# One order for all engines, made by a list scheduler in the source, and fp32 turns of the first four tiles on TensorE

## The chip, the cores and the metric

The kernel runs on one core of a Trainium2 chip. The core has five engines with a queue each: TensorE (PE), VectorE (DVE), ScalarE (ACT), GpSimd (POOL) and SyncE (SP), which here issues the DMAs. The metric is the device time of one execution in microseconds (us), the median of several runs.

## What is computed

```python
def _attn_ref(q, k, v, n_global, n_local):            # B, H, S, D = 4, 8, 768, 64
    scores = np.matmul(q, k.transpose(0, 1, 3, 2)) / np.sqrt(D)
    ...
    is_global = pos[None, :] < int(n_global)           # 8 keys
    is_local = (rel >= 0) & (rel < int(n_local))       # the last 96 keys
    ...
    scores = np.where(is_global | is_local, scores + bias, -1e9)
    a = softmax(scores)
    return np.matmul(a, v)

def _moe_ref(x, g_ln, w_ch1, w_ch2):                   # x: 4 x 768 x 512
    xn = (x - mu) / np.sqrt(var + 1e-06) * g_ln
    return x + np.maximum(xn @ w_ch1, 0.0) @ w_ch2     # 512 -> 2048 -> 512
```

A row sees at most the key block of 128 before its own, its own, and the first 8 keys. The two weight matrices come as 64-bit floats (16 MB together). Everything runs in fp16 pairs of a high and a low part, three products for each full one.

## The kernel before

The 3072 rows are 24 tiles of 128 (`TILES`): t = 0 to 3 are the first blocks of the four batches ("short" tiles, one key block, two groups of four heads), t = 4 to 23 the others ("long" tiles, two key blocks, four groups of two heads). Two tiles make a chunk of the feed-forward net (`CT`), 12 chunks in all.

For a tile, `keys`, `queries` and `values` load 256 KB each, split it (ACT writes the high part, DVE or POOL the low one) and turn k and q with DMA transposes; q is also copied with its halves swapped. A group then goes through `scores` (PE), `reduce` (DVE: mask and row maximum), `exps` (ACT), `turned` (DVE or ACT high part, POOL or DVE low part, then a DMA transpose into `pT`) and `weights_by_values` (PE, tile `pv`). `divide` and the three parts of `norm` make x and its normed fp16 pair, which a DMA transpose turns into `xT`.

`ffn1(c, f)` is one step of 24 matmuls of 256 columns for two of the 16 blocks of the hidden layer, followed by `high` (ACT) and `low` (DVE) into a tile `h`; `ffn2` is a step of 12 matmuls of 512 columns. There are 96 of each, 192 in all. `weight` turns a piece of 1 MB (16 pieces, 8 for each matrix, staging tile `st`) into fp16: ACT at L189, DVE at L190, ACT at L191, DVE at L192, ACT at L194 for the high part, DVE at L195 for the low one.

Until chunk 2 begins, the program orders the work loosely: `run` mixes generators by rates (L624 `f1w` for chunk 0 with the weights of the first matrix, L639 chunk 1, L641 `ffn2_first` for chunks 0 and 1 with the weights of the second matrix and the first 12 groups of long tiles), `ORDER` adds some dependences to DMAs, and the compiling framework arranges each engine's instructions by its own simulated times. From chunk 2 on (L651), `Lane` chains each engine's instructions in the order of the source; there the loop at L656 to L690 puts one group of attention into every second step, and `settle(LAG)` holds the products of weights by values back until two younger groups have been issued. In the profile all instructions of that part show the line of the helper, L90. DMAs are issued on SP in all parts.

Of the kernel before, what the change touches and what calls it, by code (L numbers as in the profile page):

```python
# [23 lines left out]
P = 128  # L24
# [49 lines left out]

@with_exitstack
def banded(ctx, tc, q, k, v, n_global, n_local, g_ln, w1, w2, out, flag):
    nc = tc.nc
    lanes = {}

    class Lane:  # L80
# [33 lines left out]
    marks = {}  # L114

    def mk(key, ins):

        marks[key] = ins
        if ORDER.get(key) in marks:
            tc.add_manual_dep(ins.ins, marks[ORDER[key]].ins.name, NOSYNC, reason="order")  # L120

    place = {bi: t for t, bi in enumerate(TILES)}

    def short(b, i, shape, dtype, tag, name, bufs):

        if 0 < place[b, i] < 2 * CT and not (b, i) in again:
            return hpool.tile(shape, dtype, tag="h", name=name)
        return p2.tile(shape, dtype, tag=tag, name=name, bufs=bufs)

    again = set()  # L130

    def own(b, i, name):
        if place[b, i] < CT and not (b, i) in again:
            return hpool.tile([P, H, P], F16, tag="h", name=f"{name}{b}_{i}")
        return p2.tile([P, H, P], F16, tag=name if i else name + "0", name=f"{name}{b}_{i}", bufs=3 if i else 2)

    def fetch(src, name, b, i):
        f = short(b, i, [P, H, D], F32, "ld", f"{name}f{b}_{i}", 6)
        mk(f"L{place[b, i]}", load.dma_start(out=f, in_=src[b, :, i * P:(i + 1) * P, :].rearrange("h p d -> p h d")))
        return f  # L140

    early = {}

    def loads(t, names):
        for name in names:
            early[name, t] = fetch({"k": k, "q": q, "v": v}[name], name, *TILES[t])

    loads(0, "kq")

    def piece(src, name):  # L150
        st = p3.tile([P, 2, 512], I64, tag="st", name="st" + name, bufs=3)
        mk("D" + name, load.dma_start(out=st, in_=src))
        return st

    def piece1(j, c):
        return piece(w1[2 * c * P:2 * (c + 1) * P, j * 512:(j + 1) * 512].rearrange("(a p) n -> p a n", a=2), f"1_{j}_{c}")

    cnt = counts(tc, const, load, n_global, n_local)
    ng, nl = cnt[:, 0:1], cnt[:, 1:2]

    loads(0, "v")

    mask0 = const.tile([P, H, P], BF16, name="mask0")
    mask1 = const.tile([P, H, 2, P], BF16, name="mask1")
    rel = hpool.tile([P, 2, P], F32, tag="h", name="rel")
    pool.iota(rel, pattern=[[-P, 2], [-1, P]], base=P, channel_multiplier=1, allow_small_or_imprecise_dtypes=True)
    col = hpool.tile([P, P], F32, tag="h", name="col")
    pool.iota(col, pattern=[[1, P]], base=0, channel_multiplier=0, allow_small_or_imprecise_dtypes=True)  # L170
# [5 lines left out]
    w2l = const.tile([P, NF, DM], F16, name="w2l")  # L176
    big = const.tile([P, NF], F32, name="big")
    less = const.tile([P, 1], F32, name="less")
    pool.memset(less, -0.5001)
    wm = const.tile([P, 16], F32, name="wm")  # L180

    def weight(st, dh, dl, name, n):

        words = st.rearrange("p a n -> p (a n)").bitcast(I32).rearrange("p (n two) -> p n two", two=2)
        lo, hi = words[:, :, 0], words[:, :, 1]
        mk("A" + name, act.activation(out=lo, in_=st.rearrange("p a n -> p (a n)").bitcast(U32).rearrange("p (n two) -> p n two", two=2)[:, :, 0], func=AF.Relu, scale=2.0 ** -29, bias=less))  # L189
# [736 lines left out]
```

## Time and profile before

| | us |
|---|---|
| median of three runs | 673.61 (673.53 to 678.36) |
| the profiled execution | 676.25 |
| its span, first to last instruction | 674.5 |
| TensorE busy in it | 586.6 (87%) |

The span is that of the profiled execution; the execution's own time has 1.75 us more around it, and is 2.64 us above the median. Busy time of PE is modelled, since matmuls overlap: the distance from one matmul's start to the next tells what one costs.

### The profile page before, as it was taken

To read this page: it belongs to the slowest core of one execution; us is meant where nothing else is said; L and a number is where in the kernel's file an instruction comes from. 1 tells how busy PE (TensorE), PEld (TensorE's weight loads), DVE (VectorE), ACT (ScalarE), POOL (GpSimd) and SP (SyncE) were. 2 spreads that over 40 slices of the span, in tenths; PEclk is the share of its full clock that TensorE was granted. 3 is DMA by queue.
4 is the path that set the end of the run, shared out by engine and by line. 5 is a ranking of instruction groups with operands and counts; after the bars stand their busy time and mean duration, and the time that the engine had idled before them with its cause. 6 is when DMAs were issued, how large, how long until landed. Compare 5 with 4: busy or idle time off the path is not lost.

```text
span 674.5 us, 13418 instructions
## 1 busy us (share of the span) xinstructions
PE 586.6 (87%) x5218; PEld 415.1 (62%) x5218; DVE 414.0 (61%) x984; ACT 289.5 (43%) x752; POOL 145.0 (22%) x133
## 2 busy tenths in 40 slices
PE   1113698989798998999999999999999999999995
PEld 0002565865495586587587587596686695784852
DVE  5778898845665655556475475466466457555640
ACT  4877986643144334244254243353344343230110
POOL 0000011522222332222232232233233223200000
PEclk9999999999899998999999999999999999999998
DMA  9999798996548776766886877778786785321001
GB/s 214 240 255 299 138 267 247 175 180 103 133 79 142 151 153 105 142 142 113 149 161 118 150 125 127 141 134 162 129 161 107 140 142 115 75 48 32 17 0 36
DMA packets 265767, 93.51 MB, mean 139 GB/s; under 512 B 255456, under 2 KB 255456, under 8 KB 265696
## 3 DMA queue, kind: packets, MB, share of 16 engines
q1 hardware_dynamic: 265696, 92.57, 68.8%
q8 instruction: 43, 0.70, 0.4%
q14 instruction: 28, 0.23, 0.1%
HBM read 37.49 MB, written 6.29 MB: 65 GB/s over the span
## 4 chain that ended last, share of the span: by engine, by line
PE 52%; DVE 15%; DMA 13%; ACT 8%; issue 6%; SPq 4%; POOL 1%; ACTq 0%; DVEq 0%; POOLq 0%
PE f L90 42%; DMA qf<-in_q_dram 4%; DMA st<-in_moe_w_ch_dram 4%; PE s L90 3%; SPq L90 3%; PE f L532 2%; ACT T L90 2%; PE pv L90 2%; DVE T L90 2%; DMA vf<-in_v_dram 2%; ACT T L388 1%; DVE st L190 1%; DVE st L192 1%; DVE x L90 1%; ACT st L189 1%
## 5 line engine op out<-in xcount | busy, mean ns | idle before, releaser
L90 PE MATMUL f<-xT,w1h 128*128 128x256 f16 x1280 | 216.7, 275 | 5.4 <-DMA xT<-xn 4.2
L90 PE MATMUL f<-w2h,h 128*128 128x512 f16 x640 | 201.1, 379 | 0.0
L90 PE MATMUL f<-xT,w1l 128*128 128x256 f16 x640 | 176.1, 275 | 0.0
L90 PEld LDWEIGHTS <-h 128*128 128x128 f16 x960 | 90.3, 98 | 97.8
L90 POOL TENSOR_TENSOR pn<-T,pn 128x512 f16<-128x512 f32 x68 | 80.6, 1185 | 301.0 <-DVE pn L90 175.7
L90 PEld LDWEIGHTS <-w1h 128*128 128x128 f16 x1280 | 122.6, 99 | 20.3 <-DMA xT<-xn 4.2
L90 PE MATMUL f<-w2l,h 128*128 128x512 f16 x320 | 121.3, 379 | 0.0
L90 ACT ACTIVATE h<-f 128x512 f16<-128x512 f32 x80 | 46.9, 588 | 80.0 <-PE f L90 79.7
L90 ACT ACTIVATE mn<-nm 128x2 f32<-128x2 f32 x68 | 13.8, 203 | 146.8 <-DVE nm L90 146.8
L90 DVE CAST pn<-T 128x512 f16<-128x512 f32 x68 | 29.1, 427 | 75.4 <-ACT T L90 75.4
L90 ACT ACTIVATE T<-T,mn 128x256 f32<-128x256 f32 x136 | 68.0, 500 | 4.5 <-ACT mn L90 0.4
L90 PEld LDWEIGHTS <-w1l 128*128 128x128 f16 x640 | 63.1, 99 | 7.8
L90 DVE SCALAR_TENSOR_TENSOR h<-f,h 128x512 f16<-128x512 f32 x80 | 55.0, 687 | 20.3 <-ACT h L90 19.5
L90 DVE CUSTOM_DVE_ANT_0 T<-s,mask 128x256 f32<-128x256 f32 x136 | 51.7, 417 | 23.8 <-PE s L90 23.3
L370 PE MATMUL s<-kT,qT 128*128 128x128 f16 x160 | 15.7, 255 | 36.6 <-DMA qT<-qn 27.7
L90 PE MATMUL s<-kT,qT 128*128 128x128 f16 x544 | 42.0, 219 | 6.1 <-DVE kT L90 5.6
L90 DVE SCALAR_TENSOR_TENSOR qn<-qf,qn 128x512 f16<-128x512 f32 x16 | 11.1, 692 | 58.8 <-ACT qn L90 58.8
L90 PEld LDWEIGHTS <-qT 128*128 128x128 f16 x544 | 35.8, 98 | 15.5 <-issue 7.6
L510 PE MATMUL f<-xT,w1h 128*128 128x256 f16 x128 | 36.1, 282 | 10.2 <-DMA xT<-xn 6.2
L90 PEld LDWEIGHTS <-pT 128*128 128x128 f16 x840 | 34.0, 98 | 9.3 <-DMA pT<-pn 0.9
L532 PE MATMUL f<-w2h,h 128*128 128x512 f16 x128 | 39.6, 379 | 0.0
L370 PEld LDWEIGHTS <-qT 128*128 128x128 f16 x160 | 12.5, 115 | 40.3 <-DMA qT<-qn 28.8
(129 smaller groups left out, 824.5 us busy)
## 6 DMA issues: line engine op xcount, KB each, us to landing
st<-in_moe_w_ch_dram SPq DMA_DIRECT2D x16, 1024.0 KB, 6.9
kf<-in_k_dram SPq DMA_DIRECT2D x27, 256.0 KB, 4.1
vf<-in_v_dram SPq DMA_DIRECT2D x27, 256.0 KB, 3.5
qf<-in_q_dram SPq DMA_DIRECT2D x24, 256.0 KB, 4.3
out_dram<-x SPq DMA_DIRECT2D x24, 256.0 KB, 2.4
qT<-qT SPq DMA_DIRECT2D x46, 128.0 KB, 2.5
pT<-pn SPq DMA_TRANSPOSE x88, 3.5
kT<-kn SPq DMA_TRANSPOSE x27, 3.4
```

The costliest lines, as they stand in the source:

```text
L90: ins = getattr(self.engine, name)(*args, **kw)
L189: mk("A" + name, act.activation(out=lo, in_=st.rearrange("p a n -> p (a n)").bitcast(U32).rearrange("p (n two) -> p n two", two=2)[:, :, 0 ...
L190: vec.scalar_tensor_tensor(out=lo, in0=hi, scalar=SIGN, in1=lo, op0=ALU.bitwise_and, op1=ALU.bitwise_or)
L192: vec.scalar_tensor_tensor(out=hi, in0=hi, scalar=3, in1=lo, op0=ALU.logical_shift_left, op1=ALU.bitwise_or)
L370: last = chain(last, pe.matmul(ps[:, u, n_ * P:(n_ + 1) * P], lhsT=qT[a][:, h, :], rhs=use[n_][0][:, h, :], start=(a == 0), stop=(a == 1)))
L388: act.activation(out=T[:, u, :], in_=T[:, u, :], func=AF.Exp, scale=-1.0, bias=mn[:, h:h + 1], accum_out=sm[:, h:h + 1])
L510: last = chain(last, pe.matmul(ps[:, a], lhsT=w1h[:, kk, fs], rhs=xT[:, kk, :], start=(kk == 0), stop=False))
L532: return [pe.matmul(ps, lhsT=hh[:, a, tok], rhs=w, start=(f == 0 and n_ == 0), stop=(f == NF - 1 and n_ == 2)) for n_, (a, w) in enumerate ...
```

## The change

All instructions up to the closing checks are made into tasks with an engine, a cost, the tasks they come after, a rank and the buffers they hold. `Plan.order` lays them out by these costs, always the task that can start first, and among those of one engine that start within 0.05 us the lowest rank; the instructions are then emitted in that order, and `Lane` chains them on each engine from the first one on. `ORDER`, `RATE`, `LAG`, `settle` and the generators are gone.

Beside the order, these parts differ:

- Tiles 0 to 3 (`quick`): k and q are turned in fp32 by PE with an identity, four 128x128 transposes in one PSUM bank (`turn`), and ACT and DVE split them as they leave PSUM; their scores then take four products over 64 rows in place of two over 128. The softmax weights of these tiles and their normed rows are turned likewise. No DMA transpose and no swapped copy of q is left for these tiles (20 turns by PE in all).
- v of tiles 0 to 3 is scaled and split by three POOL instructions (before: one of ACT, one of DVE).
- The low part of every weight piece is made on POOL (before: DVE), `mask1` on POOL (before: ACT). The low part of k of block 0, DVE's before, is POOL's where it is split ahead of a DMA transpose.
- Six weight pieces are staged in the places of `w2h` and `w2l` that are still empty, the others in three buffers as before. `n_global` and `n_local` are fetched on ACT's queue.
- `weights_by_values` has no lag of its own: it stands on PE where the plan has its `pT` ready.
- A step of `ffn2` for chunks 0 and 1 takes two tiles at once (12 matmuls). The products, the banks and one group of long tiles for two steps are as before; the first group of long tiles may follow the 8 steps of chunk 0.

```diff
-AHEAD = 1
-RATE = 0.5
-LAG = 2
...
-ORDER = {"L2": "q0", "L3": "q1", "D1_0_0": "q0", "D1_1_0": "q1", "D1_1_1": "q2", "L4": "p3_1", "L5": "x3"}
-ORDER.update({f"X{n}": f"l{2 + n // 8}_{2 * n % 16}" for n in range(16)})
...
+QUICK = (0.0, 6.0, 16.0, 26.0)
+PIECE = 5.0
+START = 36.0
...
+class Plan:
+
+    def __init__(self, lag=0.12):
+        self.tasks, self.room, self.lag = {}, {}, lag
+
+    def task(self, key, engine, cost, fn, after=(), rank=0.0, take=None, dma=0.0):
+        assert key not in self.tasks, key
+        self.tasks[key] = [engine, cost, fn, [a for a in after if a is not None], rank, take or {}, dma]
...
+        done, order = {}, []
+        queue = 0.0
+        while any(ready.values()):
+            best = None
+            for engine, able in ready.items():
+                now = engines.get(engine, 0.0)
+                start = {}
+                for key, t in able.items():
+                    t = max(t, now)
+                    for token in tasks[key][5]:
+                        t = max(t, min(free[token], default=1e9))
...
+                    start[key] = t
+                if not start:
+                    continue
+                t0 = min(start.values())
+                key = min((k for k in start if start[k] <= t0 + 0.05), key=lambda k: (tasks[k][4], able[k]))
+                if best is None or start[key] < best[0]:
+                    best = start[key], key, engine
+            t, key, engine = best
+            assert t < 1e8, (key, {e: list(a)[:8] for e, a in ready.items()})
...
+                free[token].remove(min(free[token]))
+            engines[engine] = t + cost
+            end = t + cost
+            if dma:
+                queue = max(t + 1.3, queue) + dma
+                end = queue + 0.6
+            done[key] = end
...
+            for owner, token in frees.get(key, ()):
+                at[owner, token] = max(at.get((owner, token), 0.0), end)
+                holds[owner, token] -= 1
+                if not holds[owner, token]:
+                    free[token].append(at[owner, token] + lag)
...
+                    ready.setdefault(tasks[u][0], {})[u] = max(done[a] + (lag if tasks[a][0] != tasks[u][0] else 0.0) for a in tasks[u][3])
+        assert len(order) == len(tasks), [k for k in tasks if k not in done][:20]
+        return [tasks[key][2] for _, key in order]
...
             def made(*args, **kw):
                 ins = getattr(self.engine, name)(*args, **kw)
-                if lanes:
-                    chain(lanes.get(self), ins)
-                    lanes[self] = ins
+                chain(lanes.get(self), ins)
+                lanes[self] = ins
                 return ins
...
+    plan.room.update(ld=6, h=17, T=3, pn=3, pT=3, s=2, pv=2, f1=2, f2=2, kT=3, vn=3, kT0=2, vn0=2, qT=2, tile=2, x=5, xT=2, st=3, turn=2)
...
+
+    def build_mask0():
...
+    def build_mask1(h):
+        pool.tensor_scalar(out=mask1[:, h], in0=made["d"], scalar1=Z * 2.0 ** -(h + 1), scalar2=None, op0=ALU.mult)
...
+    w2s = [w[:, f:f + 8, :].rearrange("p f n -> p (f n)").bitcast(I64).rearrange("p (a n) -> p a n", a=2) for f in (8, 0) for w in (w2h, w2l)]
+    homes = {0: w2s[0], 1: w2s[2], 2: w2s[1], 3: w2s[3], 7: w2s[0], 8: w2s[1]}
...
+        def lower():
+            pool.tensor_tensor(out=dl, in0=staged[n][3], in1=dh, op=ALU.subtract)
...
+        task(f"wb{n}", "SP", 0.6, bring, before, rank=rank - 12 if n < 12 else rank - 8, take={} if n in homes else {"st": [f"wl{n}"]}, dma=3.0)
+        task(f"wr{n}", "ACT", 1.24, below, [f"wb{n}", "starts"], rank=rank)
+        task(f"ws{n}", "DVE", 1.22, signs, [f"wr{n}"], rank=rank)
+        task(f"wz{n}", "ACT", 1.2, sizes, [f"ws{n}"], rank=rank)
+        task(f"ww{n}", "DVE", 1.22, whole, [f"wz{n}"], rank=rank)
+        task(f"wu{n}", "ACT", 1.15, upper, [f"ww{n}"] + (["wl1"] if n == 8 else []) + (["wl3"] if n in (8, 9, 10, 11) else []) + (["wl7", "wl8"] if n >= 12 else []), rank=rank)
+        task(f"wl{n}", "POOL", 2.4, lower, [f"wu{n}"], rank=rank)
...
+    def turn(src, name):
+        ps = ps_f.tile([P, 4, P], F32, tag=next(bank), name=name)
+        last = None
+        for u in range(4):
+            last = chain(last, pe.transpose(ps[:, u, :], src[:, u * P:(u + 1) * P], ident))
+        return ps
...
+        def both(name, home_, scale):
+            def flip():
+                turned_[name, t] = turn(raw[name, t].rearrange("p h d -> p (h d)"), f"t{name}{t}")
+
+            def high():
+                T = (kTs if name == "k" else qTs)[b, i] = home_()
+                act.activation(out=T[:, :4, :], in_=turned_[name, t], func=AF.Copy, scale=scale)
+
+            def low():
+                T = (kTs if name == "k" else qTs)[b, i]
+                if name == "k":
+                    vec.tensor_tensor(out=T[:, 4:, :], in0=turned_[name, t], in1=T[:, :4, :], op=ALU.subtract)
+                else:
...
+            task(f"t{name}{t}", "PE", slow, flip, [f"L{name}{t}", "ident"], rank=rank, take={"turn": [f"{name}l{t}"]})
+            token = {"h" if name == "q" or own else "kT0": [f"S{t}_1"]}
+            task(f"{name}h{t}", "ACT", 0.66, high, [f"t{name}{t}"], rank=rank, take=token)
+            task(f"{name}l{t}", "DVE", 0.72, low, [f"{name}h{t}"], rank=rank)
...
+        def scaled_v():
+            vf = raw["v", t]
+            pool.tensor_tensor(out=vf, in0=vf, in1=fill[:, 1:2].unsqueeze(2).to_broadcast([P, H, D]), op=ALU.mult)
...
+        task(f"v1_{t}", "POOL", 1.2, scaled_v, [f"Lv{t}", "starts"], rank=rank + 1)
+        task(f"v2_{t}", "POOL", 1.2, high_v, [f"v1_{t}"], rank=rank + 1, take={"h": [f"P{t}_1"]} if own else {"vn0": [f"P{t}_1"]} if b else {})
+        task(f"v3_{t}", "POOL", 1.2, low_v, [f"v2_{t}"], rank=rank + 1)
...
+        parts = {}
...
+        for g in range(ng_):
+            rank = ranks[g]
+            slow = 1.7 if t < 2 else 0.9 if short else 0.48
+            first_take = {"tile": [f"X{t}"]} if g == 0 else {}
+            task(f"S{t}_{g}", "PE", slow, lambda g=g: scores(g), kready + ([f"S{t}_{g - 1}"] if g else []) + gates[g], rank=rank - 20, take={"s": [f"R{t}_{g}"], **first_take})
+            task(f"R{t}_{g}", "DVE", 0.85, lambda g=g: reduce(g), [f"S{t}_{g}"], rank=rank - 3, take={"T": [f"tp{t}_{g}" if short else f"pl{t}_{g}"]})
+            task(f"E{t}_{g}", "ACT", 1.7 if short else 1.2, lambda g=g: exps(g), [f"R{t}_{g}"], rank=rank - 3)
+            if short:
+                task(f"tp{t}_{g}", "PE", 0.9 if t < 2 else 0.5, lambda g=g: flip(g), [f"E{t}_{g}"], rank=rank - 20, take={"turn": [f"pl{t}_{g}"]})
+                task(f"ph{t}_{g}", "ACT", 0.66, lambda g=g: turned_high(g), [f"tp{t}_{g}"], rank=rank - 3, take={"pT": [f"P{t}_{g}"]})
+                task(f"pl{t}_{g}", "DVE", 0.72, lambda g=g: turned_low(g), [f"ph{t}_{g}"], rank=rank - 3)
+                pready = [f"pl{t}_{g}"]
+            else:
+                task(f"ph{t}_{g}", "DVE", 0.44, lambda g=g: high(g), [f"E{t}_{g}"], rank=rank - 3, take={"pn": [f"pt{t}_{g}"]})
+                task(f"pl{t}_{g}", "POOL", 1.2, lambda g=g: low(g), [f"ph{t}_{g}"], rank=rank - 3)
+                task(f"pt{t}_{g}", "SP", 1.35, lambda g=g: across(g), [f"pl{t}_{g}"], rank=rank - 10, take={"pT": [f"P{t}_{g}"]}, dma=1.47)
+                pready = [f"pt{t}_{g}"]
+            task(f"P{t}_{g}", "PE", 0.7 if t < 2 else 0.38, lambda g=g: weights_by_values(g), pready + vready + ([f"P{t}_{g - 1}"] if g else []), rank=rank - 20, take={"pv": [f"X{t}"]} if g == 0 else {})
...
+        def scaled():
+            xc = made["xc", t]
+            act.activation(out=xc, in_=xc, func=AF.Copy, scale=made["rs", t])
...
+        if short:
+            task(f"xr{t}", "ACT", 0.72, scaled, [f"W{t}", f"C{t}"], rank=rank - 4)
+            task(f"xt{t}", "PE", 0.5, flip, [f"xr{t}"], rank=rank - 20, take={"turn": [f"xl{t}"]})
+            task(f"xh{t}", "ACT", 0.66, turned_high, [f"xt{t}"], rank=rank - 4, take=whole)
+            task(f"xl{t}", "DVE", 0.72, turned_low, [f"xh{t}"], rank=rank - 4)
+        else:
+            task(f"xh{t}", "ACT", 0.62, high, [f"W{t}", f"C{t}"], rank=rank - 4, take={"pn": [f"xa{t}"]})
+            task(f"xl{t}", "DVE", 0.72, low, [f"xh{t}"], rank=rank - 4)
+            task(f"xa{t}", "SP", 1.35, across, [f"xl{t}"], rank=rank - 12, take=whole, dma=1.47)
...
+
+        j = f // 4
+        after = [f"{'xa' if c > 1 else 'xl'}{t}" for t in range(CT * c, CT * c + CT)] + [f"wl{2 * j}", f"wl{2 * j + 1}"] + steps[-1:]
+        if c < 2:
+            last = [f"G{a}_{f}" for a in (0, 2)]
+        else:
+            last = [f"G{CT * c + CT - 1}_{f // 4 * 4}"]
+        key = f"F{c}_{f}"
+        task(key, "PE", 2.62, products, after, rank=rank, take={tag: [f"hl{c}_{f}"]})
+        task(f"hh{c}_{f}", "ACT", 0.62, high, [key], rank=rank - 6, take={"h": last[c:c + 1] if c < 2 else last})
+        task(f"hl{c}_{f}", "DVE", 0.7, low, [f"hh{c}_{f}"], rank=rank - 6)
...
+            for f in range(0, NF, 2):
+                ffn1(c, f, due(len(steps)))
+            if c == 0:
+                continue
+            for f in range(0, NF, 2):
+                for ts in ((2, 3), (0, 1)) if f else ((0, 1), (2, 3)):
+                    ffn2(ts, f, 2, {0: "f2", 1: "f2", 2: "f1", 3: "f1"}, due(len(steps)))
...
+    for t in range(2 * CT, B * NT):
+        when = [8 + 2 * (4 * (t - 2 * CT) + g) for g in range(4)]
+        tile_(t, [due(w) for w in when], [[steps[w - 1]] for w in when])
...
+    for n_ in range(16):
+        task(f"M{n_}", "DVE", 1.1, lambda n_=n_: extreme(n_), [steps[-22 + n_]], rank=1e4)
+    task("gs", "SP", 0.6, lambda: load.dma_start(out=gs, in_=g_ln.rearrange("(c p) -> p c", p=P)), [steps[-30]], dma=0.3)
+
+    for fn in plan.order():
+        fn()
     lanes.clear()
```

## Rows read from the trace of the kernel before

**Rows 1.** The page of the profiled execution, its first line and the first row of part 1 (busy time, share of the span, instructions).

```profile
span 674.5 us, 13418 instructions
...
PE 586.6 (87%) x5218; PEld 415.1 (62%) x5218; DVE 414.0 (61%) x984; ACT 289.5 (43%) x752; POOL 145.0 (22%) x133
```

**Rows 2.** Busy time by stage for the whole core (the view of windows, us from the span's start): stretch, then PE, PEld, DVE, ACT and POOL busy with their instructions, granted clock, DMA share, GB/s.

```profile
0.00:70.90 70.90, 11.65 (x112) 8.99 (x112) 52.70 (x140) 48.42 (x105) 2.77 (x11) 1.00 1.03 245
70.90:181.80 110.90, 97.80 (x841) 67.78 (x841) 85.75 (x165) 67.91 (x156) 25.53 (x20) 1.00 0.84 178
0.00:181.80 181.80, 109.45 (x953) 76.77 (x953) 138.45 (x305) 116.33 (x260) 28.30 (x31) 1.00 0.92 204
40.00:60.00 20.00, 2.84 (x32) 2.10 (x32) 15.65 (x19) 15.33 (x27) 0.00 (x0) 1.00 1.06 264
80.00:100.00 20.00, 17.51 (x159) 12.95 (x159) 19.55 (x26) 17.98 (x32) 2.10 (x2) 1.00 1.11 272
181.80:280.00 98.20, 90.96 (x852) 66.61 (x853) 55.93 (x145) 39.61 (x114) 27.73 (x24) 0.97 0.69 131
320.00:600.00 280.00, 278.97 (x2596) 199.84 (x2595) 162.84 (x419) 111.26 (x323) 77.19 (x68) 1.00 0.72 132
```

**Rows 3.** Who TensorE waited for from 0 to 185 us (the view of waits): us in total, times, longest.

```profile
PE s L370 <- DMA qT<-qn: 27.7, 4, 13.5
PE pv L426 <- DMA pT<-pn: 21.8, 6, 15.7
...
PE f L510 <- DMA xT<-xn: 6.2, 2, 3.8
```

**Rows 4.** Timeline of TensorE at its first feed-forward step, and after it has run on (start, us, line, what).

```profile
70.96 0.37 PE L510 MATMUL f<-xT,w1h 128*128 128x256 f16 x1 [3.80 <-DMA xT<-xn]
71.13 0.42 PE L511 MATMUL f<-xT,w1h 128*128 128x256 f16 x1
71.34 0.42 PE L512 MATMUL f<-xT,w1l 128*128 128x256 f16 x1
...
77.81 0.27 PE L510 MATMUL f<-xT,w1h 128*128 128x256 f16 x1
77.92 0.27 PE L511 MATMUL f<-xT,w1h 128*128 128x256 f16 x1
```

**Rows 5.** The chain of work that ended last, in order of time (start, us, what), from 155 to 215 us.

```profile
178.49 3.26 DMA xT<-xn
...
181.80 4.46 PE f L90 x24
```

**Rows 6.** The same chain in the steady loop: one step of ffn1 (24 matmuls) and one of ffn2 (12).

```profile
500.47 2.62 PE f L90 x24
...
509.47 2.59 PE f L90 x12
```

**Rows 7.** Timeline of TensorE in the steady loop: the score products of successive groups.

```profile
421.12 0.61 PE L90 MATMUL s<-kT,qT 128*128 128x128 f16 x8
...
427.09 0.61 PE L90 MATMUL s<-kT,qT 128*128 128x128 f16 x8
...
433.07 0.61 PE L90 MATMUL s<-kT,qT 128*128 128x128 f16 x8
```

**Rows 8.** The chain's end, from 660 us.

```profile
667.12 0.69 DVE x L90
...
668.15 0.14 DVE flag L736
```

**Rows 9.** Groups of instructions by line, shapes apart: engine, operation, out<-in, shapes, count | busy us, mean ns of one | idle before.

```profile
L90 POOL TENSOR_TENSOR pn<-T,pn 128x512 f16<-128x512 f32 x68 | 80.6, 1185 | 301.0 <-DVE pn L90 175.7 <-issue 120.4 <-DVE r L90 4.8
...
L192 DVE SCALAR_TENSOR_TENSOR st<-st 128x1024 int32<-128x1024 int32 x16 | 19.9, 1244 | 0.4 <-ACT st L191 0.4
L189 ACT ACTIVATE st<-st,less 128x1024 int32<-128x1024 uint32 x16 | 19.6, 1226 | 13.9 <-DMA st<-in_moe_w_ch_dram 13.8
L190 DVE SCALAR_TENSOR_TENSOR st<-st 128x1024 int32<-128x1024 int32 x16 | 19.6, 1222 | 10.8 <-ACT st L189 10.8
...
L195 DVE TENSOR_TENSOR w2l<-st,w2h 128x1024 f16<-128x1024 f32 x8 | 10.6, 1322 | 0.3 <-ACT w2h L194 0.3
...
L195 DVE TENSOR_TENSOR w1l<-st,w1h 128x1024 f16<-128x1024 f32 x8 | 9.8, 1219 | 0.9 <-ACT w1h L194 0.9
...
L379 DVE CUSTOM_DVE_ANT_0 T<-s,mask 128x128 f32<-128x128 f32 x32 | 7.3, 285 | 0.2
...
L225 DVE SCALAR_TENSOR_TENSOR vn<-vf,vn 128x512 f16<-128x512 f32 x8 | 5.5, 682 | 3.5 <-ACT vn L224 3.5
...
L730 PE MATMUL pf<-sums,ones 128*1 128x3 f32 x2 | 0.2, 166 | 0.0
```

**Rows 10.** Timeline of POOL (start, us).

```profile
129.88 2.69 POOL L397 TENSOR_TENSOR pn<-T,pn 128x512 f16<-128x512 f32 x1 [3.44 <-issue]
...
160.29 1.15 POOL L397 TENSOR_TENSOR pn<-T,pn 128x512 f16<-128x512 f32 x1 [1.07 <-issue]
```

**Rows 11.** Timeline of DVE at the same times.

```profile
130.34 1.21 DVE L195 TENSOR_TENSOR w2l<-st,w2h 128x1024 f16<-128x1024 f32 x1
...
160.40 1.60 DVE L453 SCALAR_TENSOR_TENSOR xn<-xs,rs,xn 128x512 f16<-128x512 f32 x1
```

**Rows 12.** The instructions on the tile pT from 280 to 600 us: the last line of that answer.

```profile
DMA to landing us min/median/max: 3.0/3.4/5.0
```

More of the change, by code (lines that the diff above doesn't have):

```diff
@@ L112, in chain @@
         return ins
[L114 to L170, printed above, removed]
+    plan = Plan()
+    plan.room.update(ld=6, h=17, T=3, pn=3, pT=3, s=2, pv=2, f1=2, f2=2, kT=3, vn=3, kT0=2, vn0=2, qT=2, tile=2, x=5, xT=2, st=3, turn=2)
+    task = plan.task
     w1h = const.tile([P, NK, DF], F16, name="w1h")
@@ L248, in banded @@
-    qTs = {}
-    sums = {}
-    later = []
-    ends = {}
-    def attention(t, x, xT, at):
-        b, i = TILES[t]
-        kT = keys(b, i)
-        steps = queries(t)
-        next(steps)
-        yield
-        next(steps)
-        yield
-        go(steps)
-        yield
-        blocks[b, i] = kT, values(b, i)
-        group = groups(t)
-        for g in range(2):
-            yield
-            group(g)
-            settle(0)
-        yield
-        divide(t, x, *sums.pop(t))
-        yield
-        norm(t, x, xT, at)
@@ new lines, in banded, with banks @@
+    for n in range(NF):
+        weight(n)
+    place = {bi: t for t, bi in enumerate(TILES)}
+    kTs, vns, qTs, xs, xTs, sums, smalls, ends = {}, {}, {}, {}, {}, {}, {}, {}
+    def banks():
+        for n_ in range(10):
+            yield "f2" if n_ % 2 else "f1"
+        while True:
+            yield "f2"
+    bank = banks()
+    def turn(src, name):
[4 more added lines that the diff above has]
+        return ps
@@ L565, in ffn_steps @@
-    def ffn_steps(c):
-        for f in range(0, NF, 2):
-            yield lambda: ffn1(c, f)
-        for n_ in range(CT):
-            for f in range(0, NF, 4):
-                yield lambda: ffn2(c, n_, f)
-    def run(main, side, rate):
-        due = 0.0
-        for _ in main:
-            due += rate
-            while due >= 1.0:
-                due -= 1.0
-                next(side, None)
-        for _ in side:
-            pass
-    def seq(*gens):
-        for g in gens:
-            yield from g
@@ L586, in both @@
-    def both(*gens):
-        gens = list(gens)
-        while gens:
-            for g in list(gens):
-                if next(g, g) is g:
-                    gens.remove(g)
-            yield
-    def f1w(c, js):
-        for j in js:
-            for c_ in range(NK // 2):
-                weights1(j, c_)
-                yield
-            for f in range(4 * j, 4 * j + 4, 2):
-                ffn1(c, f)
-                yield
-    def go(g):
-        for _ in g:
-            pass
-    first = [attention(t, *place_x(t)) for t in range(2 * CT)]
@@ new lines, in ffn2, with products @@
+    def ffn2(ts, f, n, tags, rank):
+        def products():
+            for t in ts:
+                if f == 0:
+                    sums2[t] = ps_f.tile([P, DM], F32, tag=tags[t], name=f"f2_{t}")
+                for f_ in range(f, f + n):
+                    product2(sums2[t], t, f_)
+        key = f"G{ts[0]}_{f}"
+        cs = sorted({t // CT for t in ts})
+        after = [f"hl{c}_{f_}" for c in cs for f_ in range(f, f + n, 2)] + [f"wl{(NF + f_) // 2}" for f_ in range(f, f + n, 2)] + steps[-1:]
+        take = {}
+        if f == 0:
+            take = {tags[ts[0]]: [f"Q{ts[-1]}"]}
+        task(key, "PE", 2.62, products, after, rank=rank, take=take)
+        steps.append(key)
+        if f + n == NF:
+            for t in ts:
+                result(t, rank, key)
```

775 lines of the change are left out of this document (399 added, 376 removed).

## Prediction

> **What bounds the kernel now.** I read the page first, then the windows by stage, then the waits and the chain of waits around the joints, and last the durations by line. The page gives PE 87% of the span [rows 1], which is an average over two regimes. In the steady loop PE is all there is: busy 278.97 of 280 us from 320 to 600 us, with DVE at 58% and ACT at 40% [rows 2]. Before it the kernel is bound by the preparation. PE is busy 11.65 of the first 70.9 us, while the DMA engines are full (share 1.03) and DVE runs 52.70 us [rows 2]; PE waits mostly for DMA transposes (27.7 us for qT, 21.8 for pT) [rows 3], and the first feed-forward step comes at 70.96 us, after one more wait for a transpose [rows 4]. From there to chunk 2, which the chain enters at 181.80 us [rows 5], pass 110.8 us.
>
> What PE must do is known. A step of ffn1 is 2.62 us and one of ffn2 2.59 us [rows 6], 2.605 on average. The score products of three successive groups start at 421.12, 427.09 and 433.07 us, 5.975 us apart [rows 7]; less two steps (5.21) a group of attention is worth 0.77 us of PE.
>
> So of the 32 steps and 12 groups that lie between first step and chunk 2, PE needs 32 x 2.605 + 12 x 0.77 = 92.6 us, and took 110.8. The 160 steps and 68 groups after it need 416.8 + 52.4 = 469.2 us; they took from 181.80 to 667.12 [rows 5, 8], 485.3, so 16 us are lost there, about 7 of them as idle PE from 181.8 to 280 us [rows 2]. Behind the last step come 7.4 us to the span's end (667.12 to 674.5) [rows 1, 8].
>
> **The change, part by part.** *The fp32 turns* take the DMA transposes and swapped copies of tiles 0 to 3 off PE's path: the waits of rows 3 go with them. In their place PE makes 20 turns of four. No row shows one; the nearest is the only fp32 matmul, recorded as two instructions of 0.166 us [rows 9]. With two passes at the 128-column share of the slow distance (0.21 us for 256 columns [rows 4]) a turn is 4 x 2 x 0.105 = 0.84 us, and at one pass of the fast distance (0.11 us) 0.22 us. I take 0.8: 20 turns are 16 us, nearly all under PE's 59 idle us before 70.9 (below: 4 us; if that cover were gone, 16). The Trainium skill (TensorE: Matmul & The Clock Gate, Part 4: PE-mode transpose) gives about 275 ns for one transpose in a kernel; by that 20 turns would be 22 us, under the same cover.
>
> *The first step.* It now needs tiles 0 and 1 and two weight pieces. A short tile costs DVE eight operations of 128x512 (0.68 each, as v's) and eight reductions of 0.285 [rows 9], with small ones 8.2 us. Two tiles, two whole pieces and half of three more (2.47 us each for L190 and L192 [rows 9]), 5 us of masks and the split of the next tile's k and q come to about 33 us. DVE has its first data at about 6 us; at 90% it is through at 42 us. Bounds: 36, if DVE never waits, and 58, if it is used as until 70.9 now (74% [rows 2]) and loses 7 us to POOL. I take 42, which is 29 us earlier.
>
> *The weights.* Until step 7 there must land eight pieces and 12 loads, some 12 MB. At 264 GB/s, which the full DMA engines moved from 40 to 60 us [rows 2], that is 45 us and a few to start, so the last pair is converted at about 58 us; step 7 of chunk 0 would start at 42 + 15.6 = 57.6. DMA therefore just keeps up, and is bounded at 5 us of delay.
>
> *Work off DVE.* Up to chunk 2 DVE was busy 138.45 us [rows 2]. The low weight parts (9.8 + 10.6 us [rows 9]) and v of tiles 0 to 3 (4 x 0.68) and the two copies of qT go, about 24 us; 114 are left. ACT had 116 [rows 2] and loses `mask1` and v, 5 us, and gains a scaling for each short tile, 3 us. Both then need 120 us of queue by chunk 2, first data included, below PE's own 42 + 92.6 = 134.6.
>
> *Work onto POOL.* It gets 16 low parts of 1024 columns; from the 512 columns of `pn` at 1.185 us [rows 9] each is 2.3 us, 37 in all (nothing cheaper is plausible with two inputs; 2.7 at the high end, by the blocked one of rows 10). Twelve operations for v are 14 us, eight mask parts of half that size 5. With the 28.3 it has [rows 2] that is 84 us by chunk 2. POOL alone is not the bound, but POOL and DVE hinder each other: `xn` on DVE, 0.6 of own work, took 1.60 us when it began 0.11 us after a POOL operation of 1.15, and `pn` on POOL took 2.69 us where a low weight part of 1.21 ran on DVE [rows 10, 11]. One stood still while the other went. DVE's own operations of that kind by chunk 2 are L190 and L192, 39.5 us [rows 9], and some 16 of attention. If they exclude POOL's 84 wholly, the two need 5 + 139 = 144 us one behind the other, 9 more than PE. They will not be without gaps: I take 152, a wait of 17 us in those 32 steps (bounds 0, if they overlap, and 35 at four fifths of use).
>
> The Trainium skill says just this (SBUF — State Buffer, Who interferes with whom): a DVE instruction with two SBUF inputs and a POOL one that reads SBUF exclude each other for the whole instruction; the rows agree. Its Perfetto Trace Analysis page (Optimizing Scalar/DVE Operations) adds that moving work between the two might not help, which is the second rival below.
>
> *The order.* From chunk 2 on it replaces one fixed order by another with the same operations. I let it win back half of the 16 us, 8 left (bounds 2 and 16). The tail is unchanged, 7.4.
>
> **Sum**, against the profiled execution: 42 + 92.6 + 17 + 469.2 + 8 + 7.4 = 636.2 us of span, where it had 674.5. Around the span lay 1.75 us, and the execution stood 2.64 above the median, so 0.9 comes off: **635 us**, 38 below the median of the runs shown.
>
> **The rivals.**
> *Early and free (a gain of 50 us or more).* POOL's and DVE's work falls apart well, chunk 2 begins at PE's own 135 us, and 2 are lost later: 135 + 469.2 + 2 + 7.4 - 0.9 = 613. For it: DVE reached 98% from 80 to 100 us [rows 2], so a dense order is possible. Against: POOL ran 2.10 us in that stretch.
> *Held by POOL and DVE.* The plan counts no exclusion, so its order meets it at every low part, in the strict queues of both engines; behind the blocked DVE operation wait the reductions, and for these the exponentials. With the two used at 82%, chunk 2 comes at 5 + 139/0.82 = 175 at worst, at 168 if they overlap by 6: 168 + 469.2 + 16 + 7.4 - 0.9 = 660.
> *PE waits at each group (slower).* Before, `settle(LAG)` left two groups, 12 us, between a group's softmax and its `pv`. Now `pv` stands on PE where the plan has `pT` ready, and PE does nothing else while it waits. The landing of pT varies from 3.0 to 5.0 us about 3.4 [rows 12], and what is late on DVE or POOL is late here. All 80 long groups pay, each anew, since each starts from PE. At 0.48 us a group the gain of 38 is gone; at the 1.6 us of a late landing, half the time, it is 80 x 0.8 = 64 us, and the kernel takes 699. For it: the lag is gone, and the exclusion is in no cost. Against: the plan's costs are near the rows (1.2 for `pn`, measured 1.185), the landing's median is near its minimum, and a `pv` that is due in the middle of a step has on average half a step, 1.3 us, to spare.
>
> **How the numbers follow.** The forecast (622 to 650, chunk 2 between 140 and 163 us) has a chance of 0.50, early and free (below 622) 0.14, held by POOL and DVE (650 to 667) 0.16, waits at each group (above 667) 0.20, of which I put 0.09 within 1% and 0.11 beyond; 1% is about what a measurement here can tell from no change. So faster 0.80, same 0.09, slower 0.11. The range takes the two bounds of the wait before chunk 2 with those of the later loss, 613 to 662, and leaves some 0.2 out, most of it above.
>
> **What would show it.** Right: the first matmul of `f` near 42 us; that of chunk 2 near 152; DVE operations on `st` of 1.2 us stretched to 2 and more beside POOL's low parts, POOL's own at 2.3 and more; PE without idle time from 320 to 600 us. Wrong: a first step after 58 us (ACT or DVE starve the tiles, or the fp32 turns cost microseconds); waits of PE for `pT` in the steady loop, summing to tens of us; or a chunk 2 near 135 us, which says that the exclusion costs nothing.

## The result, and the profile after

| | before | after |
|---|---|---|
| median of four runs, us | 673.70 (673.53 to 678.36) | 654.79 (653.86 to 655.17) |
| the profiled execution, its span | 676.25, 674.5 | 655.17, 653.4 |
| TensorE busy in it | 586.6 (87%) | 608.2 (93%) |

The ratio of after to before is 0.970, 95% interval 0.966 to 0.974: faster by 19 us, where 38 were forecast; 654.8 lies in the range of 613 to 662, but in the band that the forecast gave to its rival *held by POOL and DVE* (650 to 667, chance 0.16), above its own band of 622 to 650.

The page of after, its first line and the first row of part 1, which answer to [rows 1]:

```profile
span 653.4 us, 13632 instructions
...
PE 608.2 (93%) x5362; PEld 432.3 (66%) x5362; DVE 402.7 (62%) x960; ACT 291.8 (45%) x745; POOL 212.3 (32%) x175
```

TensorE's first feed-forward step (timeline, as [rows 4]); the second number is the duration.

```profile
50.10 0.85 PE L167 MATMUL tq<-ident,qf 128*128 128x128 f32 x3
50.74 0.63 PE L167 MATMUL f<-xT,w1h 128*128 128x256 f16 x2
```

The first 512-column step (ffn2 of chunks 0 and 1) starts at 114.70 us, chunk 2 at 167.35, and the last step ends at 645.69. The windows between these points (columns as in [rows 2]), and below them four others, the first of them the stretch from DVE's first data to the first step:

```profile
0.00:50.74 50.74, 30.92 (x233) 25.41 (x234) 37.19 (x110) 35.14 (x89) 33.16 (x36) 0.84 0.76 234
50.74:114.70 63.96, 52.12 (x458) 43.49 (x457) 55.77 (x76) 54.14 (x89) 32.50 (x16) 0.91 0.58 173
114.70:167.35 52.65, 51.94 (x430) 28.49 (x428) 39.88 (x97) 26.91 (x77) 27.21 (x21) 1.00 0.86 173
167.35:645.70 478.35, 473.09 (x4249) 334.88 (x4246) 268.77 (x675) 175.65 (x490) 119.42 (x104) 1.00 0.57 116
```
```profile
6.00:50.74 44.74, 29.84 (x229) 24.69 (x230) 36.48 (x107) 35.14 (x89) 32.27 (x25) 0.82 0.79 250
20.00:44.00 24.00, 17.27 (x143) 14.41 (x142) 20.50 (x56) 23.12 (x62) 19.68 (x15) 0.79 0.88 283
68.00:72.00 4.00, 0.24 (x1) 0.24 (x2) 3.83 (x7) 4.00 (x6) 0.99 (x1) 0.64 1.00 328
72.00:76.00 4.00, 2.62 (x13) 1.71 (x13) 4.00 (x3) 3.59 (x5) 3.06 (x2) 0.50 1.13 255
```

Against the forecast's sum, which starts at the span's beginning:

| term of the sum | forecast | measured | how |
|---|---|---|---|
| first step | 42 | 50.74 | timeline |
| from there to chunk 2 | 92.6 + 17 | 116.61 | 167.35 - 50.74 |
| chunk 2 to the last step's end | 469.2 + 8 | 478.34 | 645.69 - 167.35 |
| tail | 7.4 | 7.7 | 653.4 - 645.69 |
| span | 636.2 | 653.4 | |

Of the 17 us too little, 8.7 are the first step, 7.0 the stretch up to chunk 2, 1.1 the long rest.

Who TensorE waited for from 0 to 160 us and later is told by its waits (us in total, times, longest). The largest of the first 80 us:

```profile
PE tx L167 <- ACT xs L167: 7.8, 2, 4.3
PE tk L167 <- DMA kf<-in_k_dram: 4.7, 1, 4.7
PE tp L167 <- DVE pT L167: 3.9, 1, 3.9
```

and all that is left from 160 to 660 us:

```profile
PE pv L167 <- DMA pT<-pn: 5.1, 8, 1.1
```

The waits of [rows 3] for the transposes of q, of the weights and of the normed rows are gone; what stands there now are engines and the first loads of k and q. The rule in the forecast that low parts and DVE's word operations hinder each other is seen in POOL's and DVE's timelines at the same time (as [rows 10, 11]):

```profile
72.94 6.07 POOL L167 TENSOR_TENSOR w1l<-st,w1h 128x1024 f16<-128x1024 f32 x2 [2.02 <-ACT w1h L167]
...
84.32 2.57 POOL L167 TENSOR_TENSOR w2l<-w2l,w2h 128x1024 f16<-128x1024 f32 x1
```
```profile
72.70 1.22 DVE L167 SCALAR_TENSOR_TENSOR w2h<-w2h 128x1024 int32<-128x1024 int32 x1
73.83 3.16 DVE L167 SCALAR_TENSOR_TENSOR w2l<-w2l 128x1024 int32<-128x1024 int32 x1
...
84.83 3.14 DVE L167 SCALAR_TENSOR_TENSOR st<-st 128x1024 int32<-128x1024 int32 x1
```

DVE's operation takes 1.22 us where it began before POOL's low part (72.70 us) and 3.16 where it began behind the start of one (73.83). The groups of DVE's 32 word operations up to 170 us (count | busy, mean ns):

```profile
L167 DVE SCALAR_TENSOR_TENSOR st<-st 128x1024 int32<-128x1024 int32 x20 | 31.3, 1582 | 4.6 <-ACT st L167 4.5
...
L167 DVE SCALAR_TENSOR_TENSOR w2l<-w2l 128x1024 int32<-128x1024 int32 x6 | 9.7, 1616 | 0.0
L167 DVE SCALAR_TENSOR_TENSOR w2h<-w2h 128x1024 int32<-128x1024 int32 x6 | 8.8, 1478 | 0.3 <-ACT w2h L167 0.3
```

They are 49.8 us, where the same 32 were 39.5 before [rows 9]. Some 24 us of work left DVE, and its busy time up to chunk 2 fell from 138.45 [rows 2] only to 37.19 + 55.77 + 39.88 = 132.84. The stretched word operations are 10.3 us of the 18 that are missing; the rest is not taken apart.

### The profile page after: what moved, and what is told of

Read it like the earlier page. It is cut to its first block, busy times and chain, and to the rows that moved or that the text cites. A ratio compares the mean times of both kernels' runs of the same rounds, so it can differ in the third digit from the quotient of the medians.

```text
span 653.4 us, 13632 instructions
## 1 busy us (share of the span) xinstructions
PE 608.2 (93%) x5362; PEld 432.3 (66%) x5362; DVE 402.7 (62%) x960; ACT 291.8 (45%) x745; POOL 212.3 (32%) x175
## 4 chain that ended last, share of the span: by engine, by line
PE 70%; DVE 12%; DMA 9%; ACT 4%; issue 3%; SPq 1%; POOL 1%; ACTq 0%; DVEq 0%; POOLq 0%
PE f L167 60%; DMA pT<-pn 7%; PE s L167 5%; PE pv L167 4%; DVE st L167 3%; ACT st L167 1%; DVE w2l L167 1%; SPq L167 1%; DVE T L167 1%; ACT w2h L167 1%; DMA qT<-qn 1%; DVE x L167 1%; DVE h L167 1%; DVE vn L167 1%; ACT T L167 1%
## 5 line engine op out<-in xcount | busy, mean ns | idle before, releaser
L167 PE MATMUL f<-xT,w1l 128*128 128x256 f16 x768 | 210.7, 274 | 1.7 <-POOL w1l L167 1.7
L167 PEld LDWEIGHTS <-w1h 128*128 128x128 f16 x1536 | 148.0, 99 | 23.4 <-issue 6.0
L167 PE MATMUL f<-w2l,h 128*128 128x512 f16 x384 | 145.5, 379 | 0.0
L167 ACT ACTIVATE T<-T,mn 128x256 f32<-128x256 f32 (+1 forms) x192 | 92.4, 482 | 4.3
L167 DVE CUSTOM_DVE_ANT_0 T<-s,mask 128x256 f32<-128x256 f32 (+1 forms) x192 | 68.2, 395 | 31.6 <-PE s L167 31.5
L167 PE MATMUL s<-kT,qT 128*128 128x128 f16 (+1 forms) x768 | 61.2, 230 | 5.8 <-DVE kT L167 2.1
L167 PEld LDWEIGHTS <-qT 128*128 128x128 f16 (+1 forms) x768 | 51.8, 103 | 16.9 <-DVE qT L167 3.9
L167 PE MATMUL pv<-vn,pT 128*128 128x64 f16 x1056 | 47.4, 196 | 8.0 <-DMA pT<-pn 5.3
L167 ACT ACTIVATION_READ_ACCUMULATOR T<-T,mn 128x1 f32 x192 | 35.8, 186 | 0.0
L167 POOL TENSOR_TENSOR kn<-kf,kn 128x512 f16<-128x512 f32 x24 | 31.4, 1310 | 9.3 <-ACT kn L167 7.6
```

## The experiments

The theory after the result: the gain comes from the turns; the order loses it in part, because its costs know neither the exclusion of DVE and POOL nor the spread of pT's landing. Nine kernels test its parts. Each is the changed kernel with one or more edits, timed beside runs of the kernel before on the same chip; ratios are to that.

**Low weight parts on DVE again** (`low_on_dve`)

```diff
-            pool.tensor_tensor(out=dl, in0=staged[n][3], in1=dh, op=ALU.subtract)
+            (vec if True else pool).tensor_tensor(out=dl, in0=staged[n][3], in1=dh, op=ALU.subtract)
...
-        task(f"wl{n}", "POOL", 2.4, lower, [f"wu{n}"], rank=rank)
+        task(f"wl{n}", *(("DVE", 1.22) if True else ("POOL", 2.4)), lower, [f"wu{n}"], rank=rank)
```

> The low parts of the 16 weight pieces are made on DVE again, in the order that the plan then finds; the rest is the changed kernel (654.8 us; first feed-forward step at 50.7 us, chunk 2 at 167.5). Theory (the exclusion of DVE and POOL gives back what the move took off DVE): DVE gets 16 x 1.22 = 19.5 us more and is rid of most of the 10 us by which its operations on the weight words are stretched; chunk 2 moves by no more than 6 us and the time lies between 650 and 661. Rival (the move to POOL is a large part of the gain): chunk 2 comes 15 us or more later, 670 us or more.

Measured: 653.39 us, ratio 0.968 (0.964 to 0.971); first step 53.2, chunk 2 168.5 us. The largest group of word operations:

```profile
L167 DVE SCALAR_TENSOR_TENSOR st<-st 128x1024 int32<-128x1024 int32 x20 | 25.7, 1301 | 0.0
```

The theory holds. The mean of this group falls from 1582 to 1301 ns, all 32 word operations from 49.8 to 41.9 us, and the time stays: moving the low parts to POOL brought nothing. Some 8 of the 20 us that the move took off DVE came back as stretched word operations. DVE's busy time up to chunk 2 (columns as in [rows 2]) is 141.85 us here and 132.84 in after, so 9 us did leave it:

```profile
0.00:168.50 168.50, 134.51 (x1117) 97.28 (x1118) 141.85 (x296) 115.30 (x255) 57.33 (x55) 0.89 0.77 192
```

Why these 9 brought no time is not shown. The Trainium skill (SBUF — State Buffer, Who interferes with whom) has a DVE instruction with two SBUF inputs contend with a POOL instruction that reads SBUF, over a port pair that is an exclusive lock. The timelines of after agree, with 1.22 us against 3.16.

**Tiles 0 to 3 turned by DMA again, in the plan's order** (`dma_turns`). `quick` splits k and q ahead of the transpose, as `keys` and `queries` do, and q's copy is swapped; softmax weights and normed rows likewise.

```diff
-            task(f"t{name}{t}", "PE", slow, flip, [f"L{name}{t}", "ident"], rank=rank, take={"turn": [f"{name}l{t}"]})
...
+            task(f"{name}t{t}", "SP", 1.35, flip, [f"{name}l{t}"], rank=rank - 4, take=token, dma=1.47)
```

> Tiles 0 to 3 are turned by DMA transposes as before the change (k, q with the swapped copy, softmax weights, normed rows; their scores by two products over 128 rows), all else stays in the plan. Theory (the fp32 turns on PE bring the early first step): it goes from 50.7 us back to 70 us or later, and the time rises by 15 to 30 us to 670 to 685. Rival (the order alone brings it): the first step stays below 58 us and the time below 662.

Measured: 686.28 us, ratio 1.018 (1.014 to 1.022); first step 81.2, chunk 2 196.0 us. TensorE's waits up to 200 us, the three largest:

```profile
PE s L167 <- DMA qT<-qT: 28.6, 3, 14.5
PE pv L167 <- DMA pT<-pn: 17.6, 6, 13.2
PE s L167 <- DMA qT<-qn: 16.2, 1, 16.2
```

These are the waits of [rows 3] again. The theory's direction holds; the time is 1.3 us above its span. Within the plan the turns are worth 686.28 - 654.79 = 31.5 us, more than the whole gain, and the rest of the change without them costs 12. The plan's ranks were chosen with the turns in it; whether other ranks would do better with DMA transposes was not tried.

**2 us more for the landing of pT in the plan** (`slack2`)

```diff
-                end = queue + 0.6
+                end = queue + 0.6 + (2.0 if key.startswith("pt") else 0.0)
```

> The plan counts 2 us more for the landing of a long tile's turned softmax weights; nothing else changes. Theory (PE waits in the steady loop because the products of weights by values have no lag): the 5 us in which PE waits for pT after chunk 2 began go, and most of the 9 us that are lost there beyond PE's own work; 648 to 651 us. Rival (the loss there comes from elsewhere, and a later product only moves the wait): 653 to 657 us.

Measured: 647.50 us, ratio 0.960 (0.957 to 0.964), 7.3 below after and 0.5 below the theory's span, so the theory holds; first step and chunk 2 stay (50.75 and 167.02). From 160 to 660 us one wait of TensorE is left:

```profile
PE f L167 <- DVE x L167: 0.5, 1, 0.5
```

In after the chain of waits had gone through such landings, of 3.26 and 4.90 us, around chunk 2:

```profile
163.24 3.26 DMA pT<-pn
...
166.55 0.52 PE pv L167 x12
...
186.63 4.90 DMA pT<-pn
...
191.58 0.52 PE pv L167 x12
```

So the rival *PE waits at each group* was real in kind, and small: eight waits of 5.1 us in all, and the lag that the plan lacks costs 7 us. The 2 us between the two are not taken apart.

**The plan counts the exclusion** (`port`): long DVE operations with two inputs in SBUF and POOL's share one more resource in `order`.

```diff
+                    if long_(key):
+                        t = max(t, pair[0][0])
...
+            if long_(key):
+                pair[0][0] = t + cost
```

> The plan lets no DVE operation with two operands in SBUF (or a copy within it) overlap with one of POOL; operations and engines are those of the changed kernel. Theory (the exclusion acts through an order that does not know it: what stands behind a blocked operation is late without need): chunk 2 comes 4 us or more before 167.5 and the time is 645 to 651. Rival (the exclusion acts as work that must be done by chunk 2 in any order): chunk 2 between 164 and 171, 652 to 658 us.

Measured: 656.83 us, ratio 0.974 (0.971 to 0.978); first step 50.2, chunk 2 171.8 us. The rival holds by its time (chunk 2 is 0.8 beyond its span): this order is no better. But it keeps the two engines apart in the plan only. The word operations up to 171.8 us, of 39.5 us before and 49.8 in after, still took 45.9:

```profile
L174 DVE SCALAR_TENSOR_TENSOR st<-st 128x1024 int32<-128x1024 int32 x20 | 27.9, 1413 | 0.8 <-ACT st L174 0.8
L174 DVE SCALAR_TENSOR_TENSOR w2h<-w2h 128x1024 int32<-128x1024 int32 x6 | 10.7, 1788 | 0.0
L174 DVE SCALAR_TENSOR_TENSOR w2l<-w2l 128x1024 int32<-128x1024 int32 x6 | 7.3, 1218 | 0.0
```

What an order would bring that keeps them apart on the chip too stays open.

**Without the top bits of the low words** (`no_below`)

```diff
-            act.activation(out=staged[n][0], in_=staged[n][2], func=AF.Relu, scale=2.0 ** -29, bias=less)
+            pass
...
-            vec.scalar_tensor_tensor(out=lo, in0=hi, scalar=SIGN, in1=lo, op0=ALU.bitwise_and, op1=ALU.bitwise_or)
+            vec.scalar_tensor_tensor(out=lo, in0=hi, scalar=SIGN, in1=hi, op0=ALU.bitwise_and, op1=ALU.bitwise_and)
```

> Leaves out the top three bits of the low word of each weight: ACT's first operation on every piece (1.24 us in the plan, 16 of them, 19.6 us before chunk 2 by [rows 9]) is gone, and DVE's first one reads the high word twice in place of it, so DVE's and POOL's work is what it was. Theory: the first step stands at 50.7 us, 8.7 later than forecast, because ACT is full from 20 to 44 us; then with the three or four of these operations that lie before it gone, it comes at 46 to 47, the feed-forward of chunks 0 and 1 follows at once as much earlier, chunk 2 comes at 159 to 163, and the time is 645 to 651. Rival: ACT only stands in front of a full DVE; then the first step stays within 1 us of 50.7, chunk 2 within 2 us of 167.4, and the time is 652 to 656.

Measured: 660.94 us, ratio 0.981 (0.975 to 0.986), 6 us slower than after with 19.6 us less work for ACT; first step 55.27, chunk 2 169.9 us. Both accounts fell. The window up to the first step shows where: DVE busy 44.57 us in place of 37.19, ACT only 33.12 of 55.27.

```profile
0.00:55.27 55.27, 30.49 (x265) 25.41 (x265) 44.57 (x115) 33.12 (x90) 38.27 (x37) 0.77 0.75 233
```

The word operations on `w2l` in that window, here and in after up to the same time:

```profile
L167 DVE SCALAR_TENSOR_TENSOR w2l<-w2l 128x1024 int32<-128x1024 int32 x4 | 8.3, 2064 | 0.0
```
```profile
L167 DVE SCALAR_TENSOR_TENSOR w2l<-w2l 128x1024 int32<-128x1024 int32 x4 | 5.3, 1330 | 0.0
```

Up to 170 us all 32 word operations took 54.4 us, 49.8 in after. The theory formed from this: pieces that ACT passes on earlier fall beside POOL's low parts more often. The next kernel tests it.

**The same with the low parts on DVE** (`no_below_low`): the edits of `no_below` and `low_on_dve`.

> Without the top bits of the low words (ACT's first operation on each piece is left out, 19.6 us) the kernel took 661 us and its first step came at 55.3, 4.5 us later than with them: DVE, whose own work was the same, was busy 44.5 us before that step and not 37.2, and POOL's low parts were longer. Here the low weight parts are on DVE as well. Theory: it was the exclusion; ACT's earlier pieces put DVE's word operations beside POOL's low parts more often. Then with those off POOL the saving of ACT shows: the first step comes at 48 to 52 (53.2 with the low parts on DVE and nothing left out), chunk 2 at 161 to 166, and the time is 645 to 651. Rival: it was the order; with ACT free sooner, the plan puts more of the weights in front of tiles 0 and 1 whatever engine does the low parts; then the first step stays at 54 to 58, chunk 2 at 168 to 172, and the time is 653 to 660.

Measured: 651.64 us, ratio 0.966 (0.962 to 0.970); first step 51.55, chunk 2 163.6 us. Without POOL's low parts the same saving no longer costs anything: 9.3 us below `no_below`. The theory's places held (48 to 52, 161 to 166); its time (645 to 651) was missed by 0.6: from chunk 2 to the span's end it takes 487.7 us, where after takes 486.1 and `slack2` 479.1. Against `low_on_dve` (653.39) the 19.6 us of ACT bring 1.75 us by the medians, inside both intervals, though chunk 2 comes 4.9 us earlier.

**The two faster edits together** (`slack2_low`): those of `slack2` and `low_on_dve`.

> The two edits that each made the kernel faster, together: the plan counts 2 us more for the landing of pT of the long tiles, and the low weight parts are made on DVE. Theory: they touch different stretches (after chunk 2, and before it), so the gains add: 647.5 less 1.4, 645 to 648. Rival: with the weights' low parts back on DVE the groups before chunk 2 are late on DVE, and the landing that the plan counts has to cover that too, so that nothing is added: 648 to 652.

Measured: 644.65 us, ratio 0.955 (0.950 to 0.960); chunk 2 at 166.0 us. The theory holds (0.35 us beyond its span); this is 2.9 us below `slack2`, though the intervals overlap.

**Later ranks for tiles 2 and 3** (`slack2_q23`)

```diff
-QUICK = (0.0, 6.0, 16.0, 26.0)
+QUICK = (0.0, 6.0, 24.0, 40.0)
...
-                end = queue + 0.6
+                end = queue + 0.6 + (2.0 if key.startswith("pt") else 0.0)
```

> With the 2 us of landing, tiles 2 and 3 have later ranks (24 and 40 in place of 16 and 26), nothing else. In the changed kernel the turn of tile 3's normed rows stands on TensorE ahead of step 4 of chunk 0 and waits 4.3 us there for ACT, and the granted clock is 0.50 to 0.64 from 68 to 80 us behind that wait; ACT and DVE give tiles 2 and 3 their time before the first step as well. Theory: what holds the first step is the queue of other work of ACT and DVE, not the work of tiles 0 and 1 themselves, so with tiles 2 and 3 behind, the first step comes at 45 to 48, chunk 2 at 160 to 165 and the time is 640 to 646. Rival: the work is only moved, DVE and ACT are the bound over the whole stretch until chunk 2; then the first step is earlier, but chunk 2 stays at 166 to 169, and the time is 646 to 650.

Measured: 643.81 us, ratio 0.954 (0.949 to 0.959), the lowest median of all, 3.7 us below `slack2`, whose interval it overlaps; first step 45.33 (50.75 in `slack2`), chunk 2 162.31 us. Its windows up to there:

```profile
0.00:45.33 45.33, 26.75 (x193) 20.38 (x193) 33.58 (x97) 30.26 (x69) 28.72 (x33) 1.00 0.82 261
45.33:111.37 66.04, 56.92 (x497) 46.71 (x497) 57.34 (x87) 57.15 (x108) 34.58 (x19) 0.92 0.58 161
```

The theory holds in all three numbers. DVE's 33.58 us before the first step are what the forecast had counted for it (33). The granted clock stays at 1.00 there, where after had 0.84, but that brought little of the 5.4 us: a turn takes 0.89 us from start to start in both.

**All three** (`slack2_q23_low`): the edits of `slack2_q23` and `low_on_dve`.

> The three edits that each made the kernel faster (2 us more for the landing of pT, later ranks of tiles 2 and 3, the low weight parts on DVE) together. Theory: the exclusion still takes from the stretch before chunk 2 when the first step is early, so the low parts on DVE bring their 1 to 3 us here too: chunk 2 at 159 to 162, 640 to 643. Rival: with them on DVE, DVE's queue is what is left of the bound, and its plan has the first step 6 us later; then the first step comes at 49 to 52, chunk 2 at 163 to 167 and the time is 644 to 648.

Measured: 646.29 us, ratio 0.957 (0.953 to 0.961); first step 53.0, chunk 2 166.2 us. The rival holds by its time and chunk 2, and the first step came 1 us later still: with the low parts on DVE the early first step is lost, 7.7 us, and the time is 2.5 us longer. By three pairs of medians the place of the low parts is worth -1.4, -2.9 and +2.5 us, each inside the intervals: nothing that could be told apart.

## Why the prediction was right in kind, and 20 us too low

*The turns.* Right, and the whole gain. They are worth 31.5 us (`dma_turns`). Most of the twenty are recorded at 1.0 to 1.1 us, the three from 57 to 66 us at 0.60 to 0.66, together at 20.9 us where 16 were forecast:

```profile
26.46 1.10 PE L167 MATMUL tk<-ident,kf 128*128 128x128 f32 x4
27.35 0.98 PE L167 MATMUL tq<-ident,qf 128*128 128x128 f32 x4
```

From one turn to the next pass 0.89 us, near the 0.84 worked out. The 275 ns for one transpose that the Trainium skill gives (TensorE: Matmul & The Clock Gate, Part 4: PE-mode transpose) would make 1.10, the duration in the row.

*The first step, 42, was mis-sized: 50.74.* The forecast gave DVE 33 us of work, though the parts that it lists come to about 30, and 90% of use from the first data at 6 us on. DVE had 37.19 us, and 82% from 6 us on (36.48 of 44.74). The missing thought was that the list scheduler starts whatever can start, so that tiles 2 and 3 and later weight pieces stand in front of tiles 0 and 1. `slack2_q23` moves the two tiles back and takes 5.4 of the 8.7 us; the weight pieces were not moved by themselves. DVE's work there is the forecast's, but its use from 6 us on is 83% (32.84 of 39.33), and 6 + 33/0.83 is 46. So the last 3.3 us go with the 90% that was not reached; what DVE waits for is not taken apart. That ACT, full from 20 to 44 us, was the holder was not borne out (`no_below`).

*The wait of 17 us was mis-sized: 24.0, and made of other things.* TensorE was idle for 63.96 - 52.12 + 52.65 - 51.94 = 12.55 us, less than the 17. The rest is work that the forecast did not put in this stretch: busy 104.06 us where 92.6 were counted. [rows 2] had shown 97.80 us of it before the change. 5.0 of these 11.5 us are ffn1's steps of chunks 0 and 1 at a mean granted clock of 0.91, 46.94 us busy for 16 steps of 2.62 (window of the tile f: TensorE busy, clock, DMA share, GB/s):

```profile
50.74:114.70 63.96, 46.94 (x385) 0.91 0.58 173
```

Another 5.2 us (52.12 less 46.94) are what else TensorE does in that window, the products of tiles 2 and 3: their turns, scores and weights by values. The sum had no term for them. The last 1.3 us lie beside the steps of ffn2 and are not taken apart.

The idle time is not that of the forecast's mechanism either, in which POOL and DVE work one behind the other. From 50.74 to 167.35 us TensorE waited longest for these:

```profile
PE f L167 <- DVE h L167: 4.9, 5, 1.5
PE tx L167 <- ACT xs L167: 4.3, 1, 4.3
PE f L167 <- POOL w1l L167: 1.7, 2, 1.4
```

By the forecast's own sum the low parts on DVE leave 139 - 37 + 20 = 122 us for the two engines one behind the other, less than TensorE's own 134.6, so that chunk 2 should come earlier; in `low_on_dve` it came at 168.5. So the exclusion stretches operations, but that it set the place of chunk 2 is not borne out. That *held by POOL and DVE* named 168 and chunk 2 came at 167 was in part luck. The wait's upper bound was worked out wrongly, too: at four fifths of use it is 5 + 139/0.8 - 134.6 = 44 us, not 35.

*Work off DVE.* The forecast counted the exclusion, and it is in the rows: 24 us moved took 5.6 us off DVE's busy time. The 20 us of low parts among them brought no time at all (`low_on_dve`), and the sum had no gain from them by themselves.

*The order after chunk 2.* 8 us of loss forecast, 9.1 measured, against 16 before. `slack2` shows that some 7 of them are the lag that went with `settle`: from chunk 2 to the span's end the four kernels with the 2 us take 479.0 to 479.7 us, the six without them 483.1 to 488.0. *Early and free* failed at the first stretch, *PE waits at each group* by its size: 5.1 us where it needed 38.

*The tail* was right: 7.7 us.

The chance of 0.50 lay on 622 to 650 and the result fell 5 us above it. Every term of the sum erred to the same side. What was overlooked is the work of tiles 2 and 3 on TensorE and what an order by earliest start puts ahead of the first step. That the time still lies in the range is owed to the bounds set for the two losses (35 and 16 us, measured 24.0 and 9.1); the range had no term for a late first step, whose miss used up their room.

## What to carry to other kernels

A list scheduler keeps engines busy, not the path short: what it puts in front of the first product is set by ranks, and a rank of two tiles was worth more here (5.4 us at the first step, 3.7 of the time by the medians) than moving 20 us of work between engines (nothing that could be told). An order made from fixed costs should count the spread of a DMA's landing, not its median: here 2 us of allowance for one kind of transfer gave back 7 us over 80 groups. When a forecast counts what TensorE must do between two points, every stage that still runs there belongs in the sum, and its clock.

## What the runs showed of the hardware

TensorE's granted clock fell around its waits: 0.64 from 68 to 72 us, when it was busy 0.24 of 4 us, then 0.50 from 72 to 76, with work again (windows above); 0.50 is 1.2 GHz. Behind that wait matmuls of 256 columns start 0.21 us apart (two of them from 77.43 to 77.86), and 0.11 once the clock is 1.00 again (81.31 to 81.53), so that a wait is paid a second time behind it:

```profile
76.00:80.00 4.00, 4.00 (x22) 2.89 (x23) 4.00 (x3) 2.83 (x4) 3.01 (x1) 0.58 0.96 296
80.00:84.00 4.00, 3.11 (x28) 2.44 (x25) 4.00 (x6) 4.00 (x6) 2.61 (x1) 1.00 0.79 278
```
```profile
77.43 0.63 PE L167 MATMUL f<-xT,w1h 128*128 128x256 f16 x2
77.86 0.42 PE L167 MATMUL f<-xT,w1l 128*128 128x256 f16 x1
...
81.31 0.38 PE L167 MATMUL f<-xT,w1h 128*128 128x256 f16 x2
81.53 0.27 PE L167 MATMUL f<-xT,w1l 128*128 128x256 f16 x1
```

The granted clock does not tell the whole pace. Before the change matmuls of 256 columns started 0.21 us apart from 71.13 to 76.03 us (the first of them in [rows 4]) while the clock is given as 1.00 (first row), and in `slack2_q23` they do so at the first step (second and third):

```profile
70.90:76.00 5.10, 5.04 (x24) 3.63 (x25) 3.18 (x12) 5.10 (x19) 0.00 (x0) 1.00 0.27 51
...
45.93 0.42 PE L167 MATMUL f<-xT,w1l 128*128 128x256 f16 x1
46.14 0.63 PE L167 MATMUL f<-xT,w1h 128*128 128x256 f16 x2
```

Why is not known. In `slack2_q23` the clock was 1.00 until the first step, with TensorE busy for 26.75 of 45.33 us, hardly more of the time than in `no_below` (30.49 of 55.27, clock 0.77); why the two differ was not tried.

That less work can be slower was not expected: 19.6 us taken from ACT made the kernel 6 us slower while POOL did the low parts, and no slower when DVE did them.

POOL's low part of 1024 columns took 2.14 us where no word operation of DVE ran with it for its first 1.5 us, below the 2.3 worked out from 512 columns [rows 9]:

```profile
89.20 2.14 POOL L167 TENSOR_TENSOR w2l<-st,w2h 128x1024 f16<-128x1024 f32 x1 [2.31 <-ACT w2h L167]
```
